# A convolution and a two-product gated unit on one core: product 2 with both row halves in step over two banks, transposes behind the conv's turn, last tile stored by token blocks

## The chip, the cores and the metric

One NeuronCore of a Trainium2 chip (trn2) runs the whole program. The metric is device microseconds (us) of one execution, median of several. "Span" is the time from the first to the last instruction in the trace; it is some 1.7 us shorter than the metric. All runs below are on the record as fast ones, with a granted TensorE clock of 0.996 to 1.000, and fast runs alone are compared.

## The reference

A causal convolution of 7 taps with softmaxed weights for each of 8 heads, then `h = x @ w_in`, `g = h * cos(h)`, `out = g @ w_out`:

```python
x = np.einsum('hk,bskhg->bshg', softmax(weight), unfold(x_pad))   # 8 x 4096 tokens, 192 features, 7 taps
h = x @ w_in        # (32768, 192) @ (192, 2048)     product 1
g = h * np.cos(h)
out = g @ w_out     # (32768, 2048) @ (2048, 192)    product 2
```

## The kernel before

The program works on tiles of 512 tokens (64 of them); two tiles make a unit of 1024 tokens. A tile passes through these parts:

- The conv of a unit runs on TensorE two units ahead, one channel half in each tile. It goes through `cT<-ct`, a DMA transpose, to become the moving operand of product 1.
- Product 1 makes `h` in eight groups of 6 matmuls ("h0" to "h7"), each into an own pair of banks out of **three** (`h_pool`, which the conv shares). ScalarE takes the cosine of a group ("s0" to "s7") and VectorE multiplies it with h into `g`. Only then is the group's h buffer free.
- Product 2 contracts 2048 features. Each matmul uses 64 rows of the array, and two run at once, one on each **row half**: in this kernel's trace a pair starts together at 708.04, and near the end 32 matmuls of one half alone take 2.8 us, as long as 64 in pairs. The program never lets different row halves write one bank at the same time; the kernels are written by that rule, and no run here shows what happens without it. So half 1 works one bank behind half 0, and when the halves change banks a **turn** is handed over: the last matmul of one half signals a no-op in the sync engine's queue, and the first matmul of the other half waits for it.

```python
h_pool = ctx.enter_context(tc.tile_pool(name="h_ps", bufs=3, space=PSUM))
o_pools = [ctx.enter_context(tc.tile_pool(name=n, bufs=1, space=PSUM)) for n in ("o_p", "o_q")]
...
class Turn:
    def mark(self, *insts):
        self.nop = nc.sync.nop()          # waits for insts; stands in the sync queue, among the DMA issues
        ...
    def wait(self, *insts):               # insts wait for the no-op
        ...
...
STEPS = 2 * NF                            # 32 steps of 2 matmuls: one bank
def mm2_step(q):
    phase, i = divmod(q, STEPS)
    f, si = divmod(i, 2)
    for r in range(2):
        tt, b = divmod(phase - r, 2)      # row half 1 one bank behind row half 0
        ...
        m = nc.tensor.matmul(out=o_ps[tt, b][:, si * D : (si + 1) * D],
                             lhsT=g_tiles[tt][rows, f, s * 128 : (s + 1) * 128], rhs=wo[rows, f // 2, f % 2, :], ...)
        ...                               # Turn: marked by half 0's last step, awaited by half 1's first
def evac(t, b):
    ...
    nc.scalar.copy(o_sb[t][:, 2 * b : 2 * b + 2, :]..., o_ps.pop((t, b))[:, 0 : 2 * D])
```

The order on TensorE and ScalarE is written out by hand, for the standing tiles as below and with variants for the first four. "h1" is a group of product 1, "m7" seven steps of product 2, "c1" and "c2" the two halves of the conv, with a turn between them; "p" and "q" are points at which a bank is complete. In the new order "p" is where both banks of a tile are complete and "q" the middle of a tile.

```python
PE_ORDER = "h0 m7 c1 m6 c2 m4 h1 m7 q h2 h3 m12 h4 m10 h5 m10 h6 h7 p m8"
ACT_ORDER = "s0 ec1 ec2 s1 Q s2 s3 s4 s5 P s6 s7"
```

Of the kernel before, what the change touches and what calls it, by code (L numbers as in the profile page):

```python
# [8 lines left out]
FP32 = mybir.dt.float32  # L9
# [7 lines left out]
def kernel(  # L17
# [8 lines left out]
    nc = tc.nc  # L26
    B, S, D = x.shape
# [4 lines left out]
    T = 512  # L32
    NT = NTOK // T
    NB = T // 128
    U = 1024
    NU = NTOK // U
# [35 lines left out]
    def load_unit(u, n0=0, n1=UB, queue=nc.sync):  # L72
        if n0 == 0:
            x_tiles[u] = xin.tile([128, UB + 1, D], FP32, name="x_f")
        queue.dma_start(out=x_tiles[u][:, n0:n1, :],
                          in_=xf[u * U + n0 * 128 : u * U + n1 * 128, :].rearrange("(n p) d -> p n d", p=128))
# [119 lines left out]
    def conv_out(u, c, ps, n0, m0, m1, copy, double=False, banks=(0, 1)):  # L196

        for b in banks:
            w0 = (2 * c + b) * 2 * R
            o = ct_tiles[u][:, m0:m1, :, :, w0 : w0 + 2 * R].rearrange("p n k t w -> p (n k) t w")  # L200
            i = ps[b][:, (m0 - n0) * 2 * G : (m1 - n0) * 2 * G].rearrange("p (m t w) -> p m t w", t=1, w=2 * R)
            if double:
                copy(o, i.to_broadcast([128, (m1 - m0) * NC, 2, 2 * R]))  # L203
            else:
                copy(o[:, :, 0, :], i[:, :, 0, :])  # L205

    def ring_banks():
        h = h_pool.tile([128, 2, T], FP32, name="h")
        return [h[:, 0, :], h[:, 1, :]]
# [39 lines left out]
    def turn_unit(u, n0=0, n1=UB + 1):  # L249
        ct = ct_tiles.pop(u)  # L250
        if u not in cT:
            cT[u] = cT_pool.tile([128, UB + 1, NC, 128], BF16, name="cT")
        nc.sync.dma_start_transpose(out=cT[u][:, n0:n1].rearrange("p n c k -> p (n c) k"),
                                    in_=ct[:, n0:n1].rearrange("p n c t k -> p (n c t k)"))
        cT.pop(u - 2, None)
# [62 lines left out]
    def conv_rest():  # L318
        banks = o_banks()
        for c in range(2):  # L320
            for i in range(4):
                for prev in range(2):
                    conv_mm(0, c, [b[:, 4 * G * 2 * c :] for b in banks], i, slice(0, 128), NB + 1 - prev, UB + 1 - prev, prev,
                            start=c == 0 and prev == 0 and i % 2 == 0, stop=c == 1 and prev == 1 and i % 2 == 1)
        for b in range(2):
            for c in range(2):
                conv_out(0, c, [x[:, 4 * G * 2 * c :] for x in banks], NB, NB, UB, copies[1 - b], True, (b,))

    conv_first()
    turn_first(0)  # L330
# [31 lines left out]
    STEPS = 2 * NF  # L362

    def mm2_step(q):
        phase, i = divmod(q, STEPS)
        f, si = divmod(i, 2)
        for r in range(2):
            tt, b = divmod(phase - r, 2)
            if not 0 <= tt < NT:
                continue  # L370
            if r == 0 and i == 0:

                last = (tt, b) == (NT - 1, 1)
                o_ps[tt, b] = ring_banks()[0] if last else o_pools[b].tile([128, T], FP32, name="o_ps%d" % b)
            rows = slice(64 * r, 64 * r + 64)
            s = 2 * b + si
            m = nc.tensor.matmul(out=o_ps[tt, b][:, si * D : (si + 1) * D],  # L377
                                 lhsT=g_tiles[tt][rows, f, s * 128 : (s + 1) * 128], rhs=wo[rows, f // 2, f % 2, :],
                                 start=(r == 0 and i == 0), stop=(r == 1 and i == STEPS - 1), skip_group_check=True)
            if r == 0 and i == STEPS - 1:  # L380
                turns[tt, b] = Turn()
                turns[tt, b].mark(m)
            if r == 1 and i == 0:
                turns.pop((tt, b)).wait(m)

    def evac(t, b):
        if b == 0:
            o_sb[t] = opool.tile([128, NB, D], FP32, name="o_sb")
        nc.scalar.copy(o_sb[t][:, 2 * b : 2 * b + 2, :].rearrange("p s d -> p (s d)"), o_ps.pop((t, b))[:, 0 : 2 * D])  # L389

    def store(t, b0=0, b1=2):
        nc.sync.dma_start(out=out[t * T + b0 * 256 : t * T + b1 * 256, :].rearrange("(n p) d -> p n d", p=128),
                          in_=o_sb[t][:, 2 * b0 : 2 * b1, :])

    o_ps, o_sb, turns = {}, {}, {}




    PE_ORDER = "h0 m7 c1 m6 c2 m4 h1 m7 q h2 h3 m12 h4 m10 h5 m10 h6 h7 p m8"  # L400
    ACT_ORDER = "s0 ec1 ec2 s1 Q s2 s3 s4 s5 P s6 s7"

    PE_FIRST = ["h0a h0b h1 h2 r h3 h4 h5 d1 d2 h6 h7 c1 c2 p",
                "m8 h0 m2 h1 m11 h2 m7 h3 m4 q h4 m9 d1 d2 m7 h5 m7 h6 m1 c1 c2 m8 p h7",
                "m9 c1 m1 h0 m6 c2 m9 h1 m7 q h2 h3 m15 h4 m5 h5 m12 p h6 h7",
                "m8 c1 m6 c2 m5 h0 m9 h1 m3 h2 m1 q h3 m14 h4 m7 h5 m11 h6 h7 p m8"]
    ACT_FIRST = ["s0a s0b s1 s2 s3 s4 s5 ed1 ed2 s6 ec1 ec2 s7", "s0 s1 s2 s3 s4 ed1 ed2 s5 s6 P ec1 ec2 s7",
                 "s0 ec1 ec2 s1 Q s2 s3 s4 s5 P s6 s7", "ec1 ec2 s0 s1 Q s2 s3 s4 s5 P s6 s7"]

    HALVES = {"": (0, NB), "a": (0, NB // 2), "b": (NB // 2, NB)}  # L410
    step = 0
    for t in range(NT + 2):
        u, second = divmod(t, TPU)
        cu, cc = (u + TPU, second) if t >= TPU else (1 + t, 1)
        conv = {"c": conv_part(cu, cc, ring_banks if t else o_banks, t < TPU) if cu < NU else iter(())}
        if t < TPU:
            conv["d"] = conv_part(cu, 0, ring_banks if t else o_banks, True)
        act, done, h = (ACT_ORDER if t >= len(ACT_FIRST) else ACT_FIRST[t]).split(), set(), {}

        def flush():  # L420
            while act:
                k = act[0]
                need = {"P": "p", "Q": "q", "e": k[1:2] + "2"}.get(k[0], "h" + k[1:])
                if need not in done:
                    return
                act.pop(0)
                if k == "P" and 0 <= t - 1 < NT:
                    evac(t - 1, 0)
                elif k == "Q" and 0 <= t - 2 < NT:
                    evac(t - 2, 1)  # L430
                elif k[0] == "e":
                    next(conv[k[1]], None)
                elif k[0] == "s" and t < NT:
                    gcu(t, int(k[1]), h.pop(k[1:]), *HALVES[k[2:]])

        for k in (PE_ORDER if t >= len(PE_FIRST) else PE_FIRST[t]).split():
            if k[0] == "h" and t < NT:
                h[k[1:]] = mm1(t, int(k[1]), *HALVES[k[2:]])
            elif k[0] in conv:
                next(conv[k[0]], None)  # L440
            elif k == "r":
                conv_rest()
                turn_unit(0, NB, UB)
                load_unit(2)
                load_edges(2)
                for q in range(2):
                    nc.gpsimd.tensor_copy(out=wo[:, q * HP : (q + 1) * HP], in_=wo_f[:, q * HP : (q + 1) * HP])  # L447
            elif k[0] == "m":
                for q in range(step, step + int(k[1:])):
                    mm2_step(q)  # L450
                step += int(k[1:])
            elif k[0] == "p":
                assert step % (2 * STEPS) == 0
            elif k[0] == "q":
                assert step % (2 * STEPS) == STEPS
            done.add(k)
            flush()

            if k == "q":
                if second == 0 and t and u + 1 < NU:  # L460
                    turn_unit(u + 1)
                    mend_edges(u + 1)
                if t == 1:
                    turn_unit(1)
                    cast_unit(3)
                    mend_edges(1)
                if second == 0 and u + 3 < NU:
                    cast_unit(u + 3)
                if second == 1 and t > 1 and cu < NU:
                    double_unit(cu)  # L470
                if t == NT + 1:
                    store(NT - 1, 1, 2)
            if k == "p":
                if t < NT + 1 and 0 <= t - 2:
                    store(t - 2)
                if t == NT:
                    store(NT - 1, 0, 1)
                if second == 1 and u + 4 < NU:
                    load_unit(u + 4)
                    load_edges(u + 4)  # L480
        if t == 0:
            double_unit(1)
            load_unit(3)
            load_edges(3)
            cast_unit(2)
        if t == 1:
            double_unit(2)
# [30 lines left out]
```

## Time and profile before

| | |
|---|---|
| time, median (first 3 runs; 4 runs with the one made beside the changed kernel) | 719.25 us; 719.08 us |
| span of the profiled run | 717.4 us |
| a standing tile (mean of 58) | 10.834 us |
| first matmul of tile 1; first of tile 3 | 22.10; 44.08 us |
| end of the last product-1 group; last matmul issued; end | 704.40; 713.5; 717.4 us |

The mean of a standing tile is the distance between the first weight loads of tile 4 and tile 62 in the trace, over 58; the last two of these tiles have no conv left and take 10.46 us each, before and after. The prediction shows the busy times, the groups, the chain in order of time and the end of the timeline, and how to read them. TensorE's busy time does not tell the two kernels apart: the page of the profile says 99% both before and after, and nothing of what follows can be seen in that number. The spacing of the pieces tells it.

### The profile page before, as it was taken

The numbers are of one execution on the slowest core, as the hardware profiler recorded it, in microseconds if no ns is written. First come the engines' busy times: TensorE is split into PE (matmuls) and PEld (weight loads), VectorE is DVE, ScalarE is ACT, GpSimd is POOL, SyncE is SP. The second block draws the span as 40 slices with busy tenths as digits, with TensorE's granted clock in tenths as the row PEclk, the third lists the DMA queues.
The fourth block names the chain that finished last, engine by engine and source line by source line (L and its number), as shares of the span: only waits on it lengthen the run. The fifth ranks groups of instructions, "written<-read, shape, count | busy, mean of one in ns | idle before, by whom it ended". The sixth has DMA issues, their size and how long they took to land.

```text
span 717.4 us, 26317 instructions
## 1 busy us (share of the span) xinstructions
PE 707.9 (99%) x11827; PEld 529.9 (74%) x11827; DVE 611.5 (85%) x536; ACT 618.1 (86%) x781; POOL 149.1 (21%) x123
## 2 busy tenths in 40 slices
PE   7999999999999999999999999999999999999997
PEld 3677777777777777777777777777777777777776
DVE  7788888888888888888888888888888888888984
ACT  7888888888888888888898888888888888888883
POOL 5622112221022221022220122220122221121000
PEclk9999999999999999999999999999999999999999
DMA  8945544445534356634355534566434455424312
GB/s 216 204 101 144 145 103 115 96 122 145 144 102 118 86 132 145 127 108 114 87 146 145 122 103 109 102 144 145 111 108 100 119 145 144 105 64 93 77 46 68
DMA packets 183664, 85.24 MB, mean 119 GB/s; under 512 B 111616, under 2 KB 183168, under 8 KB 183552
## 3 DMA queue, kind: packets, MB, share of 16 engines
q1 hardware_dynamic: 183128, 82.78, 47.6%
q8 instruction: 92, 1.51, 0.9%
q0 software_dynamic: 416, 0.79, 0.8%
q14 instruction: 20, 0.16, 0.1%
q10 hardware_dynamic: 8, 0.00, 0.0%
HBM read 31.36 MB, written 25.17 MB: 79 GB/s over the span
## 4 chain that ended last, share of the span: by engine, by line
PE 96%; ACT 1%; DVE 1%; DMA 1%; POOL 0%; issue 0%; DVEq 0%; POOLq 0%
PE o_ps L377 47%; PE h L347 46%; PE h L190 3%; DMA cT<-ct 1%; ACT cs L354 1%; PE h L377 0%; DVE g L358 0%; DVE band L279 0%; DVEq L513 0%; POOL mask L128 0%; ACT mask L133 0%; ACT ct L298 0%; DVE diag L269 0%; ACT ct L203 0%; DVE cT L316 0%
## 5 line engine op out<-in xcount | busy, mean ns | idle before, releaser
L358 DVE TENSOR_TENSOR g<-h,cs 128x1024 bf16<-128x1024 f32 (+1 forms) x513 | 603.4, 1217 | 92.3 <-ACT cs L354 87.4
L354 ACT ACTIVATE cs<-h 128x1024 bf16<-128x1024 f32 (+1 forms) x513 | 511.6, 1026 | 59.2 <-PE h L347 52.0
L377 PEld LDWEIGHTS <-g 64*128 64x128 bf16 x8192 | 362.2, 94 | 85.6 <-DVE g L358 0.8
L377 PE MATMUL o_ps<-wo,g 64*128 64x192 bf16 x8128 | 424.5, 243 | 1.0 <-DVE g L358 0.5
L347 PE MATMUL h<-cT,w 64*128 64x512 bf16 (+1 forms) x3078 | 399.1, 376 | 1.7 <-DVE g L358 0.9
L347 PEld LDWEIGHTS <-w 64*128 64x128 bf16 x3078 | 154.8, 94 | 87.2 <-issue 2.5
L259 POOL COPY cT<-cT 128x144 bf16<-128x144 bf16 x31 | 9.6, 309 | 495.4 <-DMA cT<-ct 409.1
L179 POOL CAST x_bf<-x_f 128x1728 bf16<-128x1728 f32 (+1 forms) x32 | 80.6, 2519 | 8.0 <-DMA x_f<-in_x_dram 7.8
L205 ACT CAST ct<-h 128x432 bf16<-128x432 f32 x120 | 56.4, 522 | 26.4 <-PE h L190 26.4
L389 ACT COPY o_sb<-o_ps 128x384 f32<-128x384 f32 x127 | 60.1, 473 | 4.8 <-PE o_ps L377 4.8
L247 POOL COPY ct<-ct 128x1728 bf16<-128x1728 bf16 x31 | 50.5, 1630 | 18.1 <-ACT ct L205 17.8
L190 PE MATMUL h<-x_bf,band 64*128 64x216 bf16 (+1 forms) x472 | 42.7, 254 | 0.0
L190 PEld LDWEIGHTS <-band 64*128 64x128 bf16 (+1 forms) x496 | 22.1, 94 | 4.4 <-issue 1.5
L105 PE MATMUL o_ps<-zero 128*128 128x512 bf16 x12 | 4.5, 536 | 1.3 <-DVE zero L100 1.3
L377 PE MATMUL h<-wo,g 64*128 64x192 bf16 x64 | 5.8, 243 | 0.0
L105 PEld LDWEIGHTS <-zero 128*128 128x128 bf16 x15 | 1.5, 118 | 3.2 <-issue 1.6
L447 POOL CAST wo<-wo_f 128x1536 bf16<-128x1536 f32 x2 | 3.0, 1479 | 2.1 <-DMA wo_f<-in_moe_w_out_dram 2.1
L190 PE MATMUL o_ps<-x_bf,band 128*128 128x96 bf16 (+1 forms) x24 | 1.9, 223 | 0.8 <-POOL x_bf L179 0.8
L389 ACT COPY o_sb<-h 128x384 f32<-128x384 f32 x1 | 0.5, 480 | 2.4 <-PE h L377 2.4
L115 ACT ACT_TABLE_LOAD x1 | 1.3, 1283 | 1.4 <-PEq L502 1.4
L292 PE MATMUL o_ps<-x_bf,band 128*128 128x48 bf16 x32 | 1.4, 183 | 0.9 <-ACT x_bf L179 0.5
L292 PEld LDWEIGHTS <-band 128*128 128x128 bf16 x32 | 1.2, 96 | 1.6 <-POOL band L279 1.6
(48 smaller groups left out, 29.6 us busy)
## 6 DMA issues: line engine op xcount, KB each, us to landing
out_dram<-o_sb SPq DMA_DIRECT2D x63, 384.0 KB
x_f<-in_x_dram SPq DMA_DIRECT2D x31, 768.0 KB
x_f<-in_x_dram SPq DMA_DIRECT2D x31, 96.0 KB
wo_f<-in_moe_w_out_dram SPq DMA_DIRECT2D x4, 384.0 KB
x_f<-in_x_dram SPq DMA_DIRECT2D x2, 384.0 KB
w<-in_moe_w_in_dram POOLq DMA_DIRECT2D x2, 384.0 KB, 6.2
cT<-ct SPq DMA_TRANSPOSE x32
out_dram<-o_sb SPq DMA_DIRECT2D x2, 192.0 KB
```

The lines of the kernel that those rows point to most:

```text
L105: nc.tensor.matmul(out=bank, lhsT=zero[:, 0:128], rhs=zero, start=True, stop=True)
L179: copy(out=bf[u][:, n0 + o : n1 + o, :].rearrange("p n (h k r) -> p (n h) k r", k=NC, r=R), in_=x_tiles[u][:, n0:n1, :].rearrange("p n (h ...
L190: return nc.tensor.matmul(out=ps[i // 2][:, 0 : (n1 - n0) * 2 * G].rearrange("p (n k i r) -> p i n k r", n=n1 - n0, k=NC, i=2)[:, i % 2], ...
L205: copy(o[:, :, 0, :], i[:, :, 0, :])
L247: nc.gpsimd.tensor_copy(out=ct[:, n0:n1, :, 1, :], in_=ct[:, n0:n1, :, 0, :])
L259: nc.gpsimd.tensor_copy(out=cT[u][:, 0:UB, :, 0 : K - 1], in_=cT[u][:, UB].rearrange("p c (n t) -> p n c t", t=16)[:, :, :, 8 : 8 + K - 1])
L347: nc.tensor.matmul(out=h[:, i, n0 * 128 : n1 * 128], lhsT=w[rows, k, j, :], rhs=c[rows, m0 + n0 : m0 + n1, k, :], start=(k == 0), stop=(k ...
L354: nc.scalar.activation(out=cs[:, :, part], in_=h[:, :, part], func=AF.Sin, bias=math.pi / 2.0, scale=1.0)
L358: nc.vector.tensor_tensor(out=g_tiles[t][:, 2 * j : 2 * j + 2, part], in0=h[:, :, part], in1=cs[:, :, part], op=ALU.mult)
L377: m = nc.tensor.matmul(out=o_ps[tt, b][:, si * D : (si + 1) * D], lhsT=g_tiles[tt][rows, f, s * 128 : (s + 1) * 128], rhs=wo[rows, f // 2, ...
L389: nc.scalar.copy(o_sb[t][:, 2 * b : 2 * b + 2, :].rearrange("p s d -> p (s d)"), o_ps.pop((t, b))[:, 0 : 2 * D])
L447: nc.gpsimd.tensor_copy(out=wo[:, q * HP : (q + 1) * HP], in_=wo_f[:, q * HP : (q + 1) * HP])
```

## The change

Its intent: no phase with one row half alone, fewer turns, and a shorter end.

```diff
 def mm2_step(q):
-    phase, i = divmod(q, STEPS)
-    f, si = divmod(i, 2)
+    tt, i = divmod(q, 2 * STEPS)
+    half, k = divmod(i, STEPS)
+    ...                                   # last tile: si, f = divmod(k, NF), block 0 in ring banks
     for r in range(2):
-        tt, b = divmod(phase - r, 2)
+        b = half ^ r                      # both halves on one tile, swapping banks at its middle
...
+    if i == STEPS - 1:
+        turns[tt] = Turn(); turns[tt].mark(*ms)
+    if i == STEPS:
+        turns.pop(tt).wait(*ms)
...
-    nc.scalar.copy(o_sb[t]..., o_ps.pop((t, b)))
+    copies[b](o_sb[t]..., o_ps.pop((t, b)))        # bank 0 by ScalarE, bank 1 by VectorE
+def finish(t):                            # the last tile, by blocks of 128 tokens
+    for si in range(2):
+        for b in range(2):
+            copies[b](o_sb[t][:, 2 * b + si, :], o_ps.pop((t, b, si)))
+            store(t, 2 * b + si, 2 * b + si + 1, [nc.scalar, nc.sync][b])
...
-    PE_ORDER = "h0 m7 c1 m6 c2 m4 h1 m7 q h2 h3 m12 h4 m10 h5 m10 h6 h7 p m8"
-    ACT_ORDER = "s0 ec1 ec2 s1 Q s2 s3 s4 s5 P s6 s7"
+    PE_ORDER = "h0 m1 c1 m6 c2 m4 h1 m10 h2 p h3 m10 h4 m9 h5 m9 h6 m4 q h7 m11"
+    ACT_ORDER = "s0 ec1 ec2 Q s1 P s2 s3 s4 s5 s6 s7"
...
             if k == "q":
                 if second == 0 and t and u + 1 < NU:
-                    turn_unit(u + 1)               # the transpose, behind the turn of product 2
                     mend_edges(u + 1)
...
             if k == "p":
+                if second == 0 and t and u + 1 < NU:
+                    turn_unit(u + 1)               # behind the turn of the conv
```

(`turn_unit` issues the transpose; it is not a `Turn`.) Cut: the orders of the first four tiles, and the rest of the first conv, whose copies are now queued behind a cosine.

## The prediction

> **What bounds the kernel now.** I read first the busy times, then the chain that ended last by line, then the groups of instructions. The columns of a group are: line, engine, operation, output<-input, count, then busy us, mean ns of one, and the idle time before it with what ended it.
>
> ```profile
> PE 707.9 (99%) x11827; PEld 529.9 (74%) x11827; DVE 611.5 (85%) x536; ACT 618.1 (86%) x781; POOL 149.1 (21%) x123
> ...
> PE 96%; ACT 1%; DVE 1%; DMA 1%; POOL 0%; issue 0%; DVEq 0%; POOLq 0%
> ...
> L358 DVE TENSOR_TENSOR g<-h,cs 128x1024 bf16<-128x1024 f32 (+1 forms) x513 | 603.4, 1217 | 92.3 <-ACT cs L354 87.4
> L354 ACT ACTIVATE cs<-h 128x1024 bf16<-128x1024 f32 (+1 forms) x513 | 511.6, 1026 | 59.2 <-PE h L347 52.0
> L377 PE MATMUL o_ps<-wo,g 64*128 64x192 bf16 x8128 | 424.5, 243 | 1.0 <-DVE g L358 0.5
> ...
> L389 ACT COPY o_sb<-o_ps 128x384 f32<-128x384 f32 x127 | 60.1, 473 | 4.8 <-PE o_ps L377 4.8
> ```
>
> TensorE is 96% of the chain and hardly ever waits; VectorE and ScalarE have some 14% of room. A busy TensorE need not be at its peak, so I take spacings from the chain in order of time (start, us, what):
>
> ```profile
> 645.37 1.30 PE h L347 x12
> 650.60 1.30 PE h L347 x12
> 656.22 1.30 PE h L347 x12
> 661.45 1.30 PE h L347 x12
> 664.05 1.40 PE o_ps L377 x34
> ```
>
> The pattern repeats after 656.22 - 645.37 = 10.85 us: one tile of 512 tokens. A product-1 group (6 matmuls, "h") is 1.30/2 = 0.65; a product-2 step (2 matmuls, one for each row half) is 1.40/17 = 0.0825. A tile has 8 groups (5.18), 64 steps (5.28) and two half convs (0.19 each): 10.84. So the steady state is already all matmuls, and only the edges of the run can give time back. The timeline of the end (start, us, engine, line, ..., [idle before it and releaser]):
>
> ```profile
> 707.44 0.51 PE L377 MATMUL o_ps<-wo,g 64*128 64x192 bf16 x8 [0.55 <-DVE g L358]
> ...
> 708.03 2.59 PEld L377 LDWEIGHTS <-g 64*128 64x128 bf16 x63 [0.24 <-SPq L164]
> ...
> 710.86 2.58 PEld L377 LDWEIGHTS <-g 64*128 64x128 bf16 x32 [0.24 <-SPq L164]
> 710.87 2.81 PE L377 MATMUL h<-wo,g 64*128 64x192 bf16 x32
> ...
> 713.71 0.48 ACT L389 COPY o_sb<-h 128x384 f32<-128x384 f32 x1 [2.35 <-PE h L377]
> ```
>
> The last 32 matmuls belong to one row half alone and take 2.8 us, as long as 64 in pairs. TensorE waits 0.55 for the last product of VectorE and twice 0.24 for a turn. From the end of the last copy (714.19) to the end of the span (717.4) are 3.2 us for one store of 192 KB.
>
> [...] 82.5 ns a step, 1.30/6 = 217 ns a pair. A step that has lost its partner costs as much as a pair. [...] the 3.2 us after the last copy fits a mostly fixed cost, so I give half the bytes little.
>
> **The change part by part.**
>
> (1) Both row halves in step. Before, row half 1 was one bank behind row half 0: 64 x 2 + 1 = 129 phases of 32 steps. Now the halves work on two banks of the same tile and swap at the middle: 128 phases. One phase = 32 x 0.0825 = 2.64 us of TensorE time removed. The change of schedule decides where. After the last product-1 group both kernels have 96 steps left (before: 8 + 56 + 32; after: 11 + 21 + 64), so the phase is saved at the start, in tiles 1 and 2, where before the first phase ran unpaired.
>
> There it is not worth its size. Tile 1 starts at 22.10, when a DMA transpose lands; nothing in the change moves that. Before, tiles 1 and 2 end at 44.08: 21.98 us for 120 steps (8 of 128 ran before 22.10), without a gap. After, tiles 1 and 2 hold 97 steps, 4 of them before 22.10. TensorE: 2 x 5.18 + 93 x 0.0825 + 2 convs on all rows (0.47 each, from the timeline) + 0.38 = 19.4 us. But ScalarE in tile 1 has 8 cosines and four conv copies: 8 x 1.0 + 4 x 0.5 = 10.0, against 9.8 of TensorE, and VectorE in tile 2 has 8 products and a copy: 8 x 1.19 (spacing of products back to back) + 0.5 = 10.0, against 9.5. With three h buffers TensorE has to wait for them. Following the order through instruction by instruction I get waits of 0.15 to 0.55 us, 1.6 in all, and an end of tile 2 near 43.1. After it 3999 steps remain, before 4000. **Gain about 0.9 us**, not 2.3.
>
> (2) Evacuation. Each bank was copied by ScalarE, 0.473 each; now ScalarE copies one and VectorE the other, both at the end of a tile. ScalarE loses 0.47 a tile. VectorE goes from 8 x 1.19 = 9.5 to about 10.0 of 10.85, plus about 0.5 in which it stands in its queue for the last matmul of the old tile. Both banks must be free after two product-1 groups (h2, h3): 1.30 us. Following one steady tile by these durations: last step issued at 3.40, ScalarE is free at 3.87 and done at 4.33, VectorE at about 4.1, needed at 4.70. The tightest places are the h buffers for the conv and for h1, which come free 0.10 to 0.13 before TensorE wants them. So it fits, with little to spare: **0**.
>
> (3) The turn in the middle of a tile is now covered by one group (0.65) and no longer two; an uncovered turn costs 0.24, and the conv's turn, covered by six steps (0.50), shows no wait in the steady state. **0**. The transpose moves ahead, from behind the half-tile turn to behind the conv's turn. It holds the sync queue some 4.1 us, from about 1 to 5 us of the tile; the next turn in that queue comes at 9.3. **0**.
>
> (4) The last tile takes column block 0 first, in ring banks, then block 1. Ninety-six steps after the last h: last product done 2.7 us after it, needed 32 + 14 steps = 3.8 after it, so the wait of 0.55 goes; of two bare turns one is left. 7.92 + 0.24 = 8.16 against 7.92 + 1.03. **Gain 0.8 us**.
>
> (5) The last copies have 192 columns, not 384, side by side on two engines: estimated 0.31 from ScalarE's 0.473 less 192 columns at some 0.8 ns (0.473 against 1.03 for 1024 columns). Stores of 96 KB on two queues, block 0 hidden. **Gain 0.2 to 0.5**, I take 0.3.
>
> Sum: 0.9 + 0.8 + 0.3 = 2.0, so 719.25 - 2.0 = 717.2 us.
>
> **The rivals.** (a) VectorE becomes the bound of the steady state. For it: 10.0 + 0.5 of 10.85 us, and margins of 0.1. Against it: my walk through the tile closes with its queue empty before the next one. If the margins are missed by 0.05 us a tile, 62 tiles give 3 us back: 720; by 0.2, 730. (b) The whole phase is worth its 2.64 us, because ScalarE and VectorE at the start overlap better than I think: then 719.25 - 2.3 - 0.8 - 0.3 = 715.9. (c) The evacuation of both banks at one point, behind a cosine on ScalarE, holds TensorE up at every tile. The margin is 0.37 us; were it lost and 0.1 more, 6 us a run. (d) The start turns worse: copies of the conv's rest are queued behind a cosine on ScalarE and delay the transpose on which tile 1 waits. Against it: that transpose waits for VectorE's copies (15.59 to 16.60, it starts at 16.69), which stay behind the same product.
>
> **Range and chances.** (b) sets the lower end with some end-of-run luck: 715.4. A part of (a) or (c), about 0.03 us a tile, sets the upper end: 719.2. Faster by 2% would be under 704.9, below what the matmuls alone leave (62 tiles x 10.84 = 672, and 44 us of start and end): 1%. Slower by 2% needs 0.25 us more in every tile: 2%.
>
> **What would show it.** Right: tiles still 10.85 us apart; tile 3 starts near 43; no matmuls of one half alone at the end; about 8.2 us between the last product-1 group and the last matmul; waits of TensorE on VectorE's products only before 44 us, over 1 us in all. Wrong: a period over 10.88 us, with TensorE waiting for g or o_sb in the steady state (a, c); tile 1 not starting at 22.1 (d); tile 3 starting near 42 (b).

## The result

The changed kernel takes 715.73 us (median of 4 runs, 715.68 to 716.01) against 719.08 of the kernel before (4 runs). The ratio is 0.9954, 95% interval 0.9936 to 0.9971. A ratio here is the mean time of one kernel's fast runs over that of the other's of the same rounds, so not quite the ratio of the medians. The result is correct, the verdict "same" at 2%, and the time lies within the predicted range, 1.5 us under the predicted 717.2.

Busy times, chain and groups of the page of the changed kernel, with the columns of the prediction's:

```profile
PE 704.0 (99%) x11826; PEld 539.5 (76%) x11827; DVE 647.6 (91%) x601; ACT 600.7 (84%) x718; POOL 149.4 (21%) x123
...
PE 96%; DVE 1%; ACT 1%; DMA 1%; POOL 1%; issue 0%; SPq 0%; POOLq 0%
...
L360 DVE TENSOR_TENSOR g<-h,cs 128x1024 bf16<-128x1024 f32 (+1 forms) x513 | 608.6, 1218 | 29.1 <-ACT cs L356 25.2
L356 ACT ACTIVATE cs<-h 128x1024 bf16<-128x1024 f32 (+1 forms) x513 | 514.0, 1022 | 99.8 <-PE h L349 93.7
...
L404 DVE COPY o_sb<-o_ps 128x384 f32<-128x384 f32 x63 | 35.1, 558 | 26.1 <-PE o_ps L393 25.8
...
L404 ACT COPY o_sb<-o_ps 128x384 f32<-128x384 f32 x63 | 29.9, 474 | 1.6 <-PE o_ps L393 1.6
```

VectorE goes from 85% to 91% and ScalarE from 86% to 84%. The 63 copies on VectorE stand 25.8 us in its queue for a last matmul: 0.4 us each where about 0.5 was foreseen. The chain is still 96% TensorE. Now the steady state and the end, in the chain in order of time (start, us, what):

```profile
640.50 0.18 PE h L190 x4
...
651.33 0.19 PE h L190 x4
...
707.74 1.50 PE h L393 x32
709.24 1.36 PE o_ps L393 x32
710.60 0.35 DVE o_sb L414
```

From one first half of the conv to the next are 10.83 us, not 10.85. At the end both row halves work in step to the last matmul, and a copy of 192 columns takes 0.35 us. The two pieces before the copy are the last 32 of the tile's 64 steps, 16 for each column block. So the spans part as follows; every number is a difference of times that the chain or the timeline shows (the last matmul counts as issued 0.08 us, one step, after its start).

| stretch | before | after | gained | predicted |
|---|---|---|---|---|
| start to the first matmul of tile 1 | 22.10 | 21.85 | 0.25 | 0 |
| tiles 1 and 2, to the first matmul of tile 3 | 21.98 | 21.19 | 0.79 | 0.9 |
| tile 3 to the end of the last product-1 group | 660.32 | 659.15 | 1.17 | 0 |
| from there to the last matmul issued | 9.11 | 8.21 | 0.90 | 0.8 |
| from there to the end | 3.84 | 3.59 | 0.25 | 0.3 |

The three edges came near what was worked out. The 0.25 in the first row comes from a transpose that landed sooner. I take it for chance: over the eleven traces made later the same point, whose path no edit touched, lies anywhere from 21.4 to 22.4. The line that was missed is the steady state: 1.17 us where nothing was expected. Of it 0.08 is one step (3999 are left after tile 2, not 4000), 1.00 lies between the first weight loads of tile 4 and tile 62 (628.4 us before, 627.4 after), and 0.09 in tile 3, which I have not followed further.

### The profile page after: what moved, and what is told of

It is laid out like the page before. It is cut to its first block, busy times and chain, and to the rows that moved or that the text cites. A ratio compares the mean times of both kernels' runs of the same rounds, so it can differ in the third digit from the quotient of the medians.

```text
span 714.0 us, 26320 instructions
## 1 busy us (share of the span) xinstructions
PE 704.0 (99%) x11826; PEld 539.5 (76%) x11827; DVE 647.6 (91%) x601; ACT 600.7 (84%) x718; POOL 149.4 (21%) x123
## 4 chain that ended last, share of the span: by engine, by line
PE 96%; DVE 1%; ACT 1%; DMA 1%; POOL 1%; issue 0%; SPq 0%; POOLq 0%
PE o_ps L393 47%; PE h L349 45%; PE h L190 3%; DMA x_f<-in_x_dram 1%; ACT cs L356 0%; PE h L393 0%; POOL x_bf L179 0%; DVE g L360 0%; DVE band L279 0%; SPq L253 0%; POOL mask L128 0%; ACT mask L133 0%; ACT ct L298 0%; PE o_ps L190 0%; DVE diag L269 0%
## 5 line engine op out<-in xcount | busy, mean ns | idle before, releaser
L393 PE MATMUL o_ps<-wo,g 64*128 64x192 bf16 x8128 | 436.6, 243 | 1.2 <-ACT ct L205 0.6
L393 PEld LDWEIGHTS <-g 64*128 64x128 bf16 x8192 | 368.4, 94 | 86.6 <-SPq L164 1.1
L349 PE MATMUL h<-cT,w 64*128 64x512 bf16 (+1 forms) x3078 | 412.4, 376 | 1.9 <-DVE g L360 1.4
L349 PEld LDWEIGHTS <-w 64*128 64x128 bf16 x3078 | 161.1, 94 | 69.2 <-issue 3.4
L404 DVE COPY o_sb<-o_ps 128x384 f32<-128x384 f32 x63 | 35.1, 558 | 26.1 <-PE o_ps L393 25.8
L404 ACT COPY o_sb<-o_ps 128x384 f32<-128x384 f32 x63 | 29.9, 474 | 1.6 <-PE o_ps L393 1.6
L190 PEld LDWEIGHTS <-band 64*128 64x128 bf16 (+1 forms) x496 | 24.3, 94 | 8.7 <-issue 1.5
L393 PE MATMUL h<-wo,g 64*128 64x192 bf16 x64 | 3.0, 243 | 0.1
```

Source lines behind the costliest of these rows:

```text
L190: return nc.tensor.matmul(out=ps[i // 2][:, 0 : (n1 - n0) * 2 * G].rearrange("p (n k i r) -> p i n k r", n=n1 - n0, k=NC, i=2)[:, i % 2], ...
L349: nc.tensor.matmul(out=h[:, i, n0 * 128 : n1 * 128], lhsT=w[rows, k, j, :], rhs=c[rows, m0 + n0 : m0 + n1, k, :], start=(k == 0), stop=(k ...
L393: ms.append(nc.tensor.matmul(out=o_ps[tt, b, si], lhsT=g_tiles[tt][rows, f, s * 128 : (s + 1) * 128], rhs=wo[rows, f // 2, f % 2, :], star ...
L404: copies[b](o_sb[t][:, 2 * b : 2 * b + 2, :].rearrange("p s d -> p (s d)"), o_ps.pop((t, b)))
```

## The experiments

Eleven kernels ran, each with its result correct. "Tile" is the mean standing tile as above. Kernels of one call (the first four, the next four, the last three) share the runs of the kernel before, whose median was 718.74 to 718.77.

| run | time, us | ratio to before (95%) | span | tile |
|---|---|---|---|---|
| e1 before, conv one step later | 717.70 | 0.9986 (0.9974 to 0.9998) | 715.9 | 10.817 |
| e2 after, plain last tile | 717.37 | 0.9991 (0.9972 to 1.0011) | 715.6 | 10.817 |
| e3 after, transposes at the half | 770.68 | 1.0712 (1.0692 to 1.0732) | 768.6 | 11.702 |
| e4 after, both copies on ScalarE | 715.85 | 0.9960 (0.9947 to 0.9972) | 714.4 | 10.819 |
| e5 after, tile 1: conv first | 716.49 | 0.9964 (0.9949 to 0.9978) | 715.2 | 10.817 |
| e6 after, last tile: two turns | 715.37 | 0.9953 (0.9940 to 0.9966) | 713.6 | 10.817 |
| e7 e5 and e6 | 714.96 | 0.9948 (0.9935 to 0.9961) | 713.1 | 10.817 |
| e8 after, conv one step earlier | 716.48 | 0.9972 (0.9959 to 0.9985) | 714.8 | 10.834 |
| the changed kernel again | 715.98 | 0.9959 (0.9947 to 0.9971) | 714.4 | 10.817 |
| e9 after, first turn by GpSimd | 715.50 | 0.9951 (0.9939 to 0.9963) | 713.8 | 10.817 |
| e10 e5, e6 and e9 | 715.27 | 0.9948 (0.9936 to 0.9960) | 713.5 | 10.817 |

### Where 1.0 us of the steady state came from (e1, e8)

Tile by tile, the distances between first weight loads tell more than their mean. In the 56 standing tiles with a conv (4 to 59) the changed kernel takes 10.830 us in every one. The kernel before alternates: 10.863 in the even tiles and 10.832 in the odd ones, 18 ns too many in the mean.

The conv's first half needs an h buffer, which comes free when VectorE has multiplied group h6 of the tile before. In the kernel before, the timeline of VectorE and then of TensorE around one such place:

```profile
641.50 1.22 DVE L358 TENSOR_TENSOR g<-h,cs 128x1024 bf16<-128x1024 f32 x1 [0.25 <-ACT cs L354]
...
642.18 0.76 PE L377 MATMUL o_ps<-wo,g 64*128 64x192 bf16 x14
642.78 0.36 PE L190 MATMUL h<-x_bf,band 64*128 64x216 bf16 x4
```

The product ends at 641.50 + 1.22 = 642.72, the conv starts 0.06 later. The seven steps before it should take 0.58 and take 0.60. The same two lines in the changed kernel:

```profile
638.98 1.22 DVE L360 TENSOR_TENSOR g<-h,cs 128x1024 bf16<-128x1024 f32 x1 [0.17 <-ACT cs L356]
...
640.32 0.37 PE L190 MATMUL h<-x_bf,band 64*128 64x216 bf16 x4
```

Here the product ends at 640.20 and the conv starts 0.12 later. Theory A: before, the conv waited a little for that buffer. Rival B: these ns are the price of the second turn, or of the half running behind. e1 gives the kernel **before** one more step ahead of the conv:

```diff
-    PE_ORDER = "h0 m7 c1 m6 c2 m4 h1 ...
+    PE_ORDER = "h0 m8 c1 m5 c2 m4 h1 ...
```

> The kernel before, with one product-2 step more ahead of the conv's first half in the standing order (m8 c1 m5 instead of m7 c1 m6); the same work. Theory A (the 0.02 us a tile that the changed kernel saved in the steady state was a wait of the conv's first matmul for an h buffer, which VectorE released some 57 ns before that matmul could issue): one step is 82 ns, so the wait goes, the tile comes down from 10.85 to 10.83 us, and the span by about 1.1 us (717.4 to 716.3). Theory B (it is the price of the second mm2 turn of a tile, or of a row half running one bank behind): nothing changes, span 717.4 +- 0.3.

e8 does the reverse to the **changed** kernel:

```diff
-    PE_ORDER = "h0 m1 c1 m6 c2 ...
+    PE_ORDER = "h0 c1 m7 c2 ...
```

> The changed kernel with the conv's first half one step earlier (c1 m7 instead of m1 c1 m6), the reverse of the edit that helped the kernel before. Theory A (in both kernels the first conv matmul stands some 57 ns or more behind VectorE's release of its h buffer; here it issues 60 ns after that limit, and one step is 82): a wait of about 0.02 us a tile comes back, 10.85 us a tile, span longer by 1.0 to 1.4 us. Rival B (the changed kernel's 10.83 comes from its fewer turns): no change, 714.0 +- 0.3.

A holds in both directions. The mean tile went from 10.834 to 10.817 us in e1 (10.830 in every tile with a conv) and from 10.817 to 10.834 in e8 (10.862 and 10.833 by turns). I took the time from the end of the last finished product to the conv's first matmul in 55 tiles of each trace (5 to 59). Its median is 53 ns before and in e8, 117 ns after and 118 in e1; no tile is more than 5 ns off. In e8's list of waits the wait has come back by name, which the list of the kernel before does not show at all (in the timeline above the record of the seven steps runs to 642.94, past the conv's start at 642.78; the weight loads, in the same trace, stood idle from 642.70 to 642.77 only):

```profile
PEld L190 <- DVE g L360: 9.3, 28, 0.3
```

(That is idle time of the weight loads, 0.33 us each, most of it hidden behind running matmuls: it is named 28 times, in every second of the 56 tiles, and those pay some 32 ns and the others 3. Why by turns, no run shows.) e8's span is only 0.8 us longer than the changed kernel's, where A asked for 1.0 to 1.4: its tiles 4 to 61 lost 1.0, but its tile 3 had started 0.16 sooner. So this third of the gain (1.0 of 3.4 us) has nothing to do with banks or halves: one word of the order by hand gives it to the kernel before, too. e1's span is 1.4 us shorter than before's 717.4. Of this 0.37 is an earlier first matmul of tile 1.

### The last tile (e2, e6)

e2 lets the last tile go the way of all others:

```diff
-        if tt < NT - 1:
+        if tt < NT:
...
-                if t == NT + 1:
-                    finish(NT - 1)           # and evac() and store() for all NT tiles
```

> The changed kernel with its last tile treated like all others: both banks end together, copies of 384 columns, one store of 384 KB. Theory A (the last tile's own order and stores by blocks are worth over a microsecond): its first matmul waits about 0.65 us for the copies of tile 62, the copies take 0.2 us more, the store of 384 KB lands 0.5 to 1 us later than that of 96: span 1.3 to 2 us longer than the changed kernel's 714.0, so 715.3 to 716. Rival B (the end is a fixed cost of a store, and the tail gained only by having no single-half phase): 0.3 us or less.

The timeline of e2's end:

```profile
705.44 5.75 PE L393 MATMUL o_ps<-wo,g 64*128 64x192 bf16 x128 [0.58 <-ACT o_sb L404]
...
711.23 0.56 DVE L404 COPY o_sb<-o_ps 128x384 f32<-128x384 f32 x1 [5.79 <-PE o_ps L393]
```

From the last product-1 group to the last matmul it is 0.8 us longer than the changed kernel (the wait for the copies: the last tile's first matmul comes at 705.44, and at the pace of 2.64 us for 64 matmuls from 702.04 it was due at 704.68), from there to the end 0.95 longer (copies of 0.56, one store of 384 KB). That makes 1.7 of the expected 1.3 to 2: theory A. One of e2's six runs took 722.26 and the others 717.25 to 717.39; I know no reason for it.

e6 shortens the last tile further. Its turn is taken for each column block, so that 16 steps lie between every mark and its wait:

```diff
-        if i == STEPS - 1:
+        if i == STEPS - 1 or (tt == NT - 1 and i == NF - 1):
-        if i == STEPS:
+        if i == STEPS or (tt == NT - 1 and i == STEPS + NF):     # turns[tt, si]
```

> The changed kernel with the last tile's middle turn taken for each column block by itself: block 0's is marked 16 steps before it is wanted, and so is block 1's. Theory A (a bare turn costs 0.25 us, and 16 steps, 1.3 us, cover it): last h to last matmul comes down from 8.20 to 7.95 us, span 713.7. Rival B (a change of banks costs that much whoever waits): 8.20 as before.

In the timeline of e6 the third block of 32 matmuls follows the second without a gap. In the changed kernel's timeline its counterpart starts at 707.74, where the second block had begun at 706.15 and 1.32 later would have been due:

```profile
706.13 1.50 PE L393 MATMUL o_ps<-wo,g 64*128 64x192 bf16 x32
707.45 1.50 PE L393 MATMUL h<-wo,g 64*128 64x192 bf16 x32
708.77 1.50 PE L393 MATMUL o_ps<-wo,g 64*128 64x192 bf16 x32
```

The stretch came down by 0.27 us, as theory A has it: a turn without cover costs 0.25 us, and none with 16 steps over it.

### The transposes (e3)

e3 puts the transposes back behind the turn at the middle of the tile:

```diff
             if k == "q":
+                    turn_unit(u + 1)
...
             if k == "p":
-                if second == 0 and t and u + 1 < NU:
-                    turn_unit(u + 1)
```

> The changed kernel with the transposes of the even tiles issued behind the turn at the middle of a tile, where the diff found them, not behind the conv's turn. Theory A (the sync queue is held some 4.1 us by a transpose and the next turn in it has to wait): issued at 9.3 us of the tile, it holds the queue to 13.4, and the next tile's conv turn, marked at 11.8 and wanted at 12.4, comes about 1 us late in every other tile: 31 x 1.0 = some 30 us, 743 to 750. Rival B (the queue has room, the move was free as predicted): within 1 us of 715.7.

Theory A holds and my size was too small: 54.6 us over the changed kernel's span. Two lines of the timeline and one of the waits (who waited for whom: us in total, times, longest):

```profile
395.56 4.87 SPq L253 DMA_TRANSPOSE cT<-ct  x1
...
400.54 0.36 PE L190 MATMUL h<-x_bf,band 64*128 64x216 bf16 x4 [2.18 <-SPq L164]
...
PE h L190 <- SPq L164: 46.6, 29, 2.2
```

The transpose holds the sync queue for 4.87 us here, one of the longest. The conv's turn of the next tile, a no-op in that queue, has to wait until 400.43, and TensorE with it, up to 2.2 us in 29 of the tiles. Over the standing tiles it starts 9.69 us into the tile and holds the queue 4.13 us (medians), and the tile behind it takes 1.6 us longer (median; up to 4.0). I had counted 4.1 us, a start at 9.3 and 1.0 us lost: the later start gives 0.4 of the difference, and I have not taken the rest apart. So moving the transposes is no gain of its own. The new order has the half-tile turn only h7, m11, h0 and m1 ahead of the next conv (0.65 + 0.91 + 0.65 + 0.08 = 2.3 us), which a transpose of 4.1 us does not fit into; the move is what makes the new order possible.

### Who copies the banks (e4)

```diff
-        copies[b](o_sb[t]...)
+        nc.scalar.copy(o_sb[t]...)
-    ACT_ORDER = "s0 ec1 ec2 Q s1 P s2 ...
+    ACT_ORDER = "s0 ec1 ec2 s1 Q P s2 ...
```

> The changed kernel with both bank copies on ScalarE, behind the cosine s1 (VectorE does none). Theory A (a bank has 1.3 us from its last matmul to its next first one, and a cosine and two copies do not fit): the second copy ends about 0.15 us late in each tile, 62 tiles: 5 to 12 us longer, 721 to 728. Rival B (ScalarE has the room, 9.7 of 10.83 us, and the split does nothing): within 1 us of 715.7.

Theory A fell: 715.85 us, a mean tile of 10.819 (one tile takes 10.944; all others with a conv 10.830, as in the changed kernel). The timeline shows why:

```profile
643.71 0.86 ACT L404 COPY o_sb<-o_ps 128x384 f32<-128x384 f32 x2
...
644.69 1.00 PE L393 MATMUL o_ps<-wo,g 64*128 64x192 bf16 x20
```

Two copies back to back take 0.86 us, less than 2 x 0.473, and end 0.12 before the next tile's first matmul. The split over two engines is worth nothing measurable here; it costs VectorE 0.56 us a tile. (The prediction had taken 0.5.)

### What cuts the gain at the start (e5, e7, e9, e10)

The phase saved is worth 2.64 us of matmuls, of which 27 steps, 2.2 us, fall between the first matmuls of tile 1 and tile 3. The change saved 0.79 there. The changed kernel's waits up to 46 us offer two reasons:

```profile
PEld L393 <- SPq L164: 0.8, 1, 0.8
...
PE h L349 <- DVE g L360: 0.5, 1, 0.5
```

Theory A (the prediction's): TensorE is held by the loop of three h buffers through ScalarE and VectorE. Rival B: the first tile's turn stands in the sync queue behind a transpose of 5.36 us, from 23.58 to 28.94, and TensorE waits 0.8 us for it. The prediction had put that wait at 0. e5 moves one word, so that the conv covers the wait:

```diff
-    "... h5 m2 q m1 d1 d2 m4 h6 ..."
+    "... h5 m2 q d1 d2 m5 h6 ..."
```

> The changed kernel with one word of tile 1's order moved: the conv d1 d2 directly behind the half-tile mark, ahead of the step that waits for the turn (the trace of the changed kernel shows that wait as 0.79 us at 28.25, behind a transpose that holds the sync queue until 28.94). Theory A (the gain of the start, 1.04 us of the phase's 2.64, is cut by the loop of h buffers through ScalarE and VectorE): the wait shrinks to under 0.35 us but h6 still waits for VectorE's fifth product, and tile 3 starts only 0.1 to 0.3 us sooner than 43.04. Rival B (the turn behind the transpose cut it): tile 3 starts 0.5 to 0.8 us sooner.

e7 joins the edits of e5 and e6:

> Both of the two last edits together. If each theory A holds: 0.1 to 0.3 us from the start and 0.25 from the end, span 713.4 to 713.7, time 715.1 to 715.4; with rival B of the start 712.9 to 713.2.

e5 was inconclusive. In its profiled run the transpose took 6.61 us and the wait grew to 1.6 (of the weight load, as the 0.8 above), and its four runs spread from 715.22 to 717.20. e7 has the same edit. Tile 3 started 0.57 us sooner than in the changed kernel, but tile 1 had started 0.44 sooner. From the first group of tile 1 to the first group of tile 2 it took 11.28 us. The six traces that share the changed kernel's start (the changed kernel twice, e2, e4, e6, e8) have 11.32 to 11.65, mean 11.46. That speaks for A, but too softly. So e9 takes the turn out of the sync queue altogether:

```diff
-            turns[tt].mark(*ms)
+            turns[tt].mark(*ms, queue=nc.sync if tt else nc.gpsimd)
```

and the changed kernel runs beside it once more, unaltered:

> The changed kernel once more, unaltered, on the chip and in the rounds of the next two: 715.2 to 716.2 us. Tile 1 lasts (first h of tile 1 to first h of tile 2) 11.3 to 11.7 us, as in the five traces that share its start.

> The changed kernel with the turn of tile 0 alone (the one that waited 0.5 to 1.0 us behind a transpose in the sync queue) handed through GpSimd's queue, which is between two casts then. The wait for the sync queue in tile 1 should be gone. Theory A (the h loop through ScalarE and VectorE cuts the start nearly as far): h6 then waits for VectorE instead and tile 1 shortens by only 0.1 to 0.3 us, from 11.4 to about 11.2. Rival B (the turn behind the transpose cut it): it shortens by 0.5 to 0.8 us, to 10.6 to 10.9; without any wait it would be 10.2.

The wait for the sync queue is gone, 0.3 us for GpSimd's is left, and tile 1 takes 11.24 us: 0.2 less than the mean of those six, where B asked for 0.5 to 0.8. The timeline of e9 (VectorE, then TensorE's group h6):

```profile
28.57 2.36 DVE L360 TENSOR_TENSOR g<-h,cs 128x1024 bf16<-128x1024 f32 x2 [0.21 <-ACT cs L356]
...
29.84 0.82 PE L349 MATMUL h<-cT,w 64*128 64x512 bf16 x6
```

The first of the two products, the tile's fifth, ends about 29.8 and group h6, which takes over its buffer, starts at 29.84. In the changed kernel it started at 30.05. The buffer loop stands right behind the turn. Theory A holds: removing the turn's wait lets the loop set the pace.

Last, e10 puts the edits of e5, e6 and e9 together:

> The changed kernel with the three edits of e5, e6 and e9. The end gains 0.25 to 0.3 us as in e6; the start 0.2 to 0.4 with theory A, 0.6 to 1.0 with rival B. Time 0.4 to 0.7 us (A) or 0.9 to 1.3 us (B) under the changed kernel in the same rounds.

It confirms it once more: tile 1 takes 11.24 us, but tile 2 gives 0.19 back (10.89 against 10.70 from its first group to that of tile 3), with 0.9 us of waits for VectorE up to 46 us, not 0.5. That list leaves out short ones. So I also looked in tiles 1 and 2 for matmuls that start later after the one before them than the pace of 0.22 us a pair or 0.08 a step. In the changed kernel three are late by more than 0.15 us:

```profile
25.04 0.82 PE L349 MATMUL h<-cT,w 64*128 64x512 bf16 x6
...
29.05 0.26 PE L393 MATMUL o_ps<-wo,g 64*128 64x192 bf16 x2 [0.56 <-SPq L164]
...
36.52 0.82 PE L349 MATMUL h<-cT,w 64*128 64x512 bf16 x6 [0.48 <-DVE g L360]
```

The first comes 0.25 us late and the third 0.64, each just after a product of VectorE has ended; the second, behind the turn, comes 0.72 late. In e10 no turn is waited for, and three such waits for VectorE's products make 1.5 us (0.25, 0.53 and 0.69): the loop takes up nearly all that the turn gave free.

In the same rounds e10 is 0.7 us under the changed kernel (715.27 to 715.98), e7 in its own rounds has the same ratio, 0.9948. These two beat both kernels, by about 0.1% over the changed one. Of that 0.27 us is shown (the last tile's turns); the rest is within the spread of the start.

## Why the prediction was right, and where not

**The time and range.** Right: 715.73 in 715.4 to 719.2. It lies near the lower end, and the main reason is one term, found by no working of mine: without its 1.0 us the time would have been some 716.7, 0.5 under the prediction.

**"[T]he steady state is already all matmuls, and only the edges of the run can give time back."** This step failed. It compared a sum of spacings (10.84) with a period read to 0.01 us (10.85) and took the rest for rounding. The rest was a wait in the tiles with a conv, some 33 ns in every second one and 2 in the others, 1.0 us in all, which the new order removed by luck: nothing in the prediction aimed at it. (The pieces add up to 10.83 where nothing waits, not 10.84.) Two things hid it. The list of waits did not name it (the matmul records overlap there, by 0.16 us in the place shown), and the margins of 0.10 to 0.13 us for the h buffers were worked out for the new order only. The same walk through the old order should have shown it at its limit; I have not redone it. For the new order the margins were rightly called small: 117 - 53 = 64 ns at the conv where 0.10 us was worked out, and e8 shows that one step (82 ns) more than uses it up.

**(1) In step.** Right in kind and size: 0.79 measured for 0.9, tile 3 at 43.04 for "near 43.1", and e9 and e10 show that the buffer loop through VectorE is what withholds the rest. The waits of "1.6 in all" are 1.6 in the trace too, but 0.7 of them is the turn in tile 1, which the prediction left out; for VectorE it is 0.9, under the "over 1 us" that was to show it right. Without that turn the loop would have taken nearly as much (1.5 in e10), so the sum came out right.

**(2) Evacuation.** Right: no wait on a bank in any standing tile (all 56 with a conv take 10.830 us). e4 shows that the split over two engines was not even needed; the prediction left that open.

**(3) Turns and transposes.** In the standing tiles right. The "0" for the transpose's move was argued from "the next turn in that queue comes at 9.3", and e3 shows how dear that queue is: 54.6 us a run for turns behind transposes. In tile 1 the new order has just such a turn, and there the step was wrong.

**(4) and (5) The end.** Right: 8.21 us to the last matmul where 8.16 was worked out, and 0.25 us for the smaller copies and stores where 0.3 was. From the end of the last copy to the end of the span it is 3.2 us with 192 KB in the last store (before), 3.0 with 96 on each of two queues (after) and 3.8 with 384 (e2): mostly fixed over these sizes, as the prediction took it. e2 undoes both and loses 1.7, more than 0.8 + 0.3, since a plain tile in step also meets a wait for the old banks that the kernel before did not have.

**Rivals.** (a) and (c) did not come about, (d) neither: tile 1 started at 21.85. (b), the whole phase, is refuted by 0.79; that the time landed near its 715.9 has another cause.

**Left open:** why e5's runs spread over 2 us when e7, with the same edit in tile 1, kept within 0.5; how much of e7's and e10's gain over the changed kernel lies in the start; and why the conv's wait fell on every second tile.

## What to carry to other kernels

Where an engine is 96% of the chain, compare the period with the sum of its pieces to a few ns, over many tiles: a wait of some 33 ns that the list of waits did not name, repeated in every second tile, was a third of this gain, and moving one step of the order removed it without any new structure (e1). A signal sent through the sync queue waited here for the DMA transpose ahead of it in that queue, 0.8 us in tile 1 and up to 2.2 us in 29 tiles of e3; place a signal by what is issued before it in its queue, and look for a transpose above all. When a wait has been found at the start or the end, ask which one stands right behind it before counting its length as a gain.

## What these runs measured

- How long a DMA transpose holds the queue that issues it: 4.0 to 5.0 us (median 4.1) for one of 27x128 columns in the standing tiles of the kernels before and after, and up to 6.6 for the first whole one, near the start (e5). The turns behind it in the queue waited for it (e3: 54.6 us a run).
- The price of a hand-over from one matmul to a later one through the sync queue: with nothing over it, it cost 0.25 us (e6 took one away and gained 0.27).
- What ended a gap that repeats on the busiest engine: here such a gap, 18 ns a tile in the mean, was a wait for a PSUM buffer, but it took no further buffer to end it. 82 ns of other matmuls put ahead of it removed it (e1) and taken away brought it back (e8). The list of waits of the kernel before does not name this gap; the spacing of the tiles showed it.
- A copy of 384 fp32 columns out of PSUM: 558 ns on VectorE and 474 on ScalarE. Two ScalarE copies back to back took 0.86 us (e4), less than twice the one.
